# Packed attention followed by a gated MLP on one Trainium2 core: three bursts of small matmul tiles per batch instead of four, and one copy moved ahead of a table load

## The chip, the core and the metric

One core of one Trainium2 chip runs the whole program. The metric is the device time of one execution in microseconds (us). Five engines work side by side, each through its own instruction stream in order: TensorE (PE) multiplies, VectorE (DVE), ScalarE (ACT) and GpSimd (POOL) work elementwise, SyncE (SP) issues DMA transfers; POOL issues some too. They wait for each other by semaphores. PE writes its results to PSUM, which is eight banks of 2 KB in each of 128 partitions; everything else lies in SBUF. Before a weight tile is used PE loads it, which the profile shows as a row of its own (PEld).

## The reference, cut to what matters

```python
batch, n_heads, seq, head_dim, n_pack = 8, 8, 576, 64, 32
n_tokens, d_model, d_ff = 4608, 512, 2048

def sm_attn(qq, kk, vv):
    s = scale * np.matmul(qq, kk.transpose(0, 1, 3, 2))
    s = s - np.max(s, axis=-1, keepdims=True)
    a = np.exp(s)
    a = a / (np.sum(a, axis=-1, keepdims=True) + 1e-09)
    return np.matmul(a, vv)

p_packed = sm_attn(p, k, v)              # 32 packed rows per head
attn = sm_attn(q, p_packed, p_packed)    # every token attends to them
x = attn.transpose(0, 2, 1, 3).reshape(4608, 512)
h = x @ w_in
out = (h * np.cos(h)) @ w_out
```

q, k and v are 8 x 8 x 576 x 64, p is 8 x 8 x 32 x 64, w_in 512 x 2048 and w_out 2048 x 512, all fp32.

## The kernel before

The kernel works batch by batch (B = 8) and computes in bf16 with fp32 sums. It never forms x: since each token's attention output is a weighted sum of 32 packed rows per head, it multiplies the packed rows by w_in first (**PPW**, 256 x 2048 per batch) and then the attention weights by PPW, which gives h directly.

For one batch the steps are, with the helper's name:

- `s1`: scores of p against k, 16 small matmuls (64 rows by 32 columns of the array), and exp with its row sums on ACT. `recips` takes the reciprocals.
- `a1_xbar` (a DMA transpose from SP's queue) or `a1_pe` (PE transposes): the weights transposed.
- `pp` (L173): the packed rows, 48 small matmuls of 96 rows by 32 columns, into one PSUM bank, and two copies of it to `pp_sb`. `pp_T` (L188): two transposes of that and a copy to `ppT`.
- `ppw(b, n)` (L195): chunk n of PPW (512 of its 2048 columns), 8 small matmuls of 64 by 32 into both banks of a PSUM tile, and a copy to SBUF. A batch needs four. `pw2(b, n)` is `ppw(b, n)` and `ppw(b, n + 1)`.
- `s2`: scores of q against the packed rows (16 small matmuls), exp on ACT; `sums2` and `normalise`: row sums by a matmul with ones, their logarithm, exp of the negative, and the product on DVE (`a2n`).
- `h_mm(b, fc)` (L248), for fc = 0 to 15: 128 of the 2048 rows of h. Four full-size matmuls into columns 0 to 287 of both banks of one PSUM tile, cosine on ACT (`Sin` with a bias, L258), product on DVE (L261) into `gT`. It reads PPW chunk fc // 4.
- `out_gen(b)`: the product with w_out, 16 full-size matmuls (L339) for each chunk of 128 tokens. A batch's 576 tokens are four chunks and a half; two halves are put together in `joint` and belong to the odd batch, so an even batch has four chunks and an odd one five. For batch 0 the 64 rest columns of h are done by `h_rest` (L286).

**What sets the order.** Everything is written out by hand in program order (`manual_schedule`); semaphores between engines follow from who reads and writes which tile, and in PSUM by bank. While batch s goes through `h_mm`, the output matmuls of batch s - 1 are dealt out between, as *filler*: `fill(n)` issues the next n of them. `slot(s, hooks, keep, heavy)` (L471) runs the sixteen `h_mm` of a batch. It shares the filler that is left, less `keep`, by weights (1 for each fc, plus what `heavy` adds), and runs the small steps given as hooks at their fc: at a heavy fc half of the quota goes before the hooks and half behind them, elsewhere all of it behind.

**PSUM.** Two banks (`O`, tag ot) are for the output. The other six are `psA`, three tiles of two banks each, which `h_mm`, `ppw`, `s1`, `s2`, `sums2`, `pp` and `pp_T` all draw from by `psa()`; a new tile waits until the last reader of the old one is done. For batch 0 the six banks are single tiles instead (`psH`, by `one()`), used by `h_one` (L274), the variant of `h_mm` with 512 columns.

**ACT's tables.** Exp and logarithm need one table set, Sin another; the kernel loads them by hand (`preload_act_table_set`), twice per batch.

**The parts that the change touches.** The start (L440 to L470): the sixteen `h_one` of batch 0, then `pp_T(1)`, the exp table, three groups of PE transposes of q of batch 1 (`pe_T`, copied by ACT, DVE, DVE), `s2(1)` and what follows. The first slot (L496), the middle between slots 1 and 2 (L506 to L541), the second slot (L542) and the loop over s = 3 to 7 (L545). In the loop small tiles come at four places per batch: `s2(s)` with `ppw(s, 2)`; `s1(s + 1)` with `ppw(s, 3)`; `pp(s + 1)` at fc 5 of the slot; and `pw2(s + 1)`, chunks 0 and 1 of the next batch, at fc 10.

Of the kernel before, what the change touches and what calls it, by code (L numbers as in the profile page):

```python
# [15 lines left out]
def kernel(  # L16
# [18 lines left out]
    HS = S // 2  # L35
# [53 lines left out]
    def psa(dt=FP32):  # L89
        return psum["A"].tile([128, 2, 512 if dt == FP32 else 1024], dt, name="psA", tag="A")  # L90
# [12 lines left out]
    def pe_T(n, b, engs=(V, V, V), groups=(0, 1, 2), own=None):  # L103
        if 0 in groups:
            xT[n, b] = att_pool.tile([128, H * 3, TP], BF16, name=n + "T", tag=n + "T", bufs=2 if n == "k" else 1)
        t = xT[n, b]
        flat = bf[n, b].rearrange("p h x -> p (h x)")
        for i in groups:
            ps = own(BF16) if own else psa(BF16)[:, 0, :]
            for j in range(8):  # L110
                o = 8 * i + j
                nc.tensor.transpose(ps[:, j * TP:(j + 1) * TP], flat[:, o * 128:(o + 1) * 128],
                                    ident[0:TP, 0:TP])
            copy(engs[i], t[:, 8 * i:8 * i + 8].rearrange("p a x -> p (a x)"),
                 ps[:, 0:8 * TP])
# [79 lines left out]
    def ppw(b, n, eng=None, own=False, later=False, cuts=((0, 512),)):  # L195
        if b not in PPW:
            PPW[b] = ppw_pool.tile([128, 2, DF], BF16, name="PPW", tag="PPW")
        two = isinstance(eng, tuple)
        if own:
            ps = [bank(), bank()]  # L200
        else:
            t = psa()
            ps = [t[:, 0, :], t[:, 1, :]]
        for x in range(4):
            for y in range(2):
                r = slice(64 * y, 64 * y + 64)
                nc.tensor.matmul(ps[y][32 * x:32 * x + 32, :], ppT[b % 2][r, 0, x, :],  # L207
                                 w_in_bf[r, x, n * 512:(n + 1) * 512], start=True, stop=True)

        def evacuate(cuts=cuts):  # L210
            if own or two:
                for a, z in cuts:
                    for y in range(2):
                        copy(eng[y] if two else eng, PPW[b][:, y, n * 512 + a:n * 512 + z], ps[y][:, a:z])
            else:
                copy(eng or (V, ACT)[n % 2], PPW[b][:, :, n * 512:(n + 1) * 512], t)
        if later:
            return [lambda c=c: evacuate((c,)) for c in cuts]
        evacuate()
# [25 lines left out]

    gT, joint = {}, {}

    def h_mm(b, fc):  # L248
        if fc == 0:
            g_tile(b)  # L250
        ps = psa()
        for y in range(2):
            for e in range(2):
                nc.tensor.matmul(ps[:, e, 0:HS], PPW[b][:, y, fc * 128:(fc + 1) * 128],  # L254
                                 a2n[b][:, y, e * HS:(e + 1) * HS], start=(y == 0), stop=(y == 1))
        cs = cos_pool.tile([128, S], BF16, name="cosT")
        csv = cs.rearrange("p (e x) -> p e x", e=2)
        ACT.activation(out=csv, in_=ps[:, :, 0:HS], func=AF.Sin, bias=PI_HALF)  # L258

        def rest():  # L260
            V.tensor_tensor(out=gT[b][:, fc, :].rearrange("p (e x) -> p e x", e=2),  # L261
                            in0=ps[:, :, 0:HS], in1=csv, op=ALU.mult)
            if fc % 8 == 7:
                j0 = (b % 2) * 64
                G.tensor_copy(out=joint[b // 2][:, fc - 7:fc + 1, j0:j0 + 64],  # L265
                              in_=gT[b][:, fc - 7:fc + 1, 512:576])
        return rest
# [3 lines left out]
        if b % 2 == 0:  # L271
            joint[b // 2] = j_pool.tile([128, NFC, 128], BF16, name="joint", tag="joint")

    def h_one(b, fc):  # L274

        if fc == 0:
            g_tile(b)
        ps = one()
        for y in range(2):
            nc.tensor.matmul(ps, PPW[b][:, y, fc * 128:(fc + 1) * 128], a2n[b][:, y, 0:512],  # L280
                             start=(y == 0), stop=(y == 1))
        cs = cos_pool.tile([128, 512], BF16, name="cosT")
        ACT.activation(out=cs, in_=ps, func=AF.Sin, bias=PI_HALF)  # L283
        V.tensor_tensor(out=gT[b][:, fc, 0:512], in0=ps, in1=cs, op=ALU.mult)  # L284

    def h_rest(b):  # L286

        t = psa()
        for fc in range(NFC):
            for y in range(2):  # L290
                nc.tensor.matmul(t[:, fc // 8, (fc % 8) * 64:(fc % 8) * 64 + 64],
                                 PPW[b][:, y, fc * 128:(fc + 1) * 128], a2n[b][:, y, 512:576],
                                 start=(y == 0), stop=(y == 1))
        cs = cos_pool.tile([128, 2, 512], BF16, name="cosR", bufs=1)
        ACT.activation(out=cs, in_=t, func=AF.Sin, bias=PI_HALF)
        j0 = (b % 2) * 64
        V.tensor_tensor(out=joint[b // 2][:, :, j0:j0 + 64],
                        in0=t.rearrange("p a (f x) -> p (a f) x", x=64),
                        in1=cs.rearrange("p a (f x) -> p (a f) x", x=64), op=ALU.mult)
# [55 lines left out]
    def fill(n):  # L355
        while n > 0 and filler[1] > 0:
            next(filler[0])
            filler[1] -= 1
            n -= 1
# [13 lines left out]
    def warm(n, wps=None, w=None):  # L373
        wps, w = bank() if wps is None else wps, wz if w is None else w
        for _ in range(n):
            nc.tensor.matmul(wps, w[:, 0:128], w, start=True, stop=True)  # L376
# [61 lines left out]
    a1_pe(1, own=one)  # L438
    recips(1)
    for fc in range(NFC):  # L440
        h_one(0, fc)
        if fc in (0, 4, 8):
            ppw(0, 1 + fc // 4, (ACT, ACT if fc == 8 else V), own=True)
        if fc == 13:
            pp(1, ACT, own=bank)
    warm(2)
    pp_T(1, ACT, own=bank)
    warm(2)
    ACT.preload_act_table_set(EXP_SET)  # L449
    pe_T("q", 1, (ACT, V, V), own=one)  # L450
    warm(4)
    load("v", 2)
    load("q", 2)
# [3 lines left out]
    set_filler(0)  # L457
    s2(1)
    ppw(1, 0, V)
    fill(1)  # L460
    sums2(1, 0)
    fill(1)
    sums2(1, 1)
# [7 lines left out]
    def slot(s, hooks, keep=0, heavy={}):  # L471
        left = filler[1] - keep
        weight = [1 + heavy.get(fc, 0) for fc in range(NFC)]
        for fc in range(NFC):
            h_mm(s, fc)()
            quota = (left * sum(weight[:fc + 1])) // sum(weight) - (left + keep - filler[1])
            first = quota
            while hooks and hooks[0][0] == fc:
                if first == quota and fc in heavy:
                    first = quota // 2  # L480
                    fill(first)
                hooks.pop(0)[1]()
            fill(quota - first if first != quota else quota)

    def pw2(b, n=0, eng=None):
        ppw(b, n, eng)
        ppw(b, n + 1, eng)

    def tk(n, b, i):
        return lambda: pe_T(n, b, (ACT, V, ACT), (i,))  # L490

    def cross(n, b):
        return lambda: xbar(n, b)

    osb_eng[0] = ACT
    slot(1, [(2, lambda: ppw(1, 2, (ACT, V))), (4, lambda: h_rest(0)),  # L496
             (5, lambda: ppw(1, 3, (ACT, V))), (6, lambda: pack_p(2, 4)), (8, tk("k", 2, 0)), (9, tk("k", 2, 1)),
             (9, cross("q", 2)), (10, tk("k", 2, 2)), (12, cross("k", 3))], 4, {4: 2})
    ACT.preload_act_table_set(EXP_SET)
    osb_eng[0] = V  # L500
    G.tensor_copy(out=gate, in_=xT["k", 3][0:1, 0, 0:1])
# [11 lines left out]
    recips(2)  # L513
    fill(5)
    pp(2)
    fill(2)
    pp_T(2)
    s1(3)
    a1_xbar(3)
    recips(3)  # L520
    fill(6)
    s2(2)
# [15 lines left out]
    for n, b in (("v", 4), ("q", 4), ("k", 5)):  # L538
        load(n, b)
    fill(9)  # L540
    osb_eng[0] = ACT  # L541
    slot(2, [(3, lambda: ppw(2, 2, (ACT, V))), (6, lambda: ppw(2, 3, (ACT, V))),  # L542
             (7, lambda: pp(3, ACT)), (8, lambda: pp_T(3, ACT)), (11, lambda: pw2(3))], 5, {11: 3})

    for s in range(3, B):  # L545
        nxt = s + 1 < B
        ACT.preload_act_table_set(EXP_SET)
        osb_eng[0] = V
        fill(1000)
        set_filler(s - 1)  # L550
        s2(s)
        ppw(s, 2, V)
        fill(8)
        if nxt:
            s1(s + 1)
            ppw(s, 3, V)
            a1_xbar(s + 1)
            xbar("q", s + 1)
            recips(s + 1)
            if s + 2 < B:  # L560
                xbar("k", s + 2)
                G.tensor_copy(out=gate, in_=xT["k", s + 2][0:1, 0, 0:1])
        else:
            ppw(s, 3, V)
        fill(4)
        sums2(s, 0)
        fill(5)
        sums2(s, 1)
        normalise(s)
        ACT.preload_act_table_set(SIN_SET)  # L570
        fill(13)
        osb_eng[0] = ACT
        for n, b in (("v", s + 2), ("q", s + 2), ("k", s + 3)):
            if b < B:
                load(n, b)
        slot(s, [(5, lambda: pp(s + 1, ACT)), (6, lambda: pp_T(s + 1, ACT)), (10, lambda: pw2(s + 1))] if nxt else [], 5, {10: 3})
    set_filler(B - 1)
    fill(1000)
    tail_chunk(B - 1, 4)
# [30 lines left out]
```

## Time and profile before

| | us |
|---|---|
| median of 3 runs | 249.57 (249.48 to 250.11) |
| the profiled execution | 249.53 |
| its span, first to last instruction | 247.6 |
| PE busy | 234.0 |
| ACT busy | 170.3 |
| DVE busy | 158.5 |
| matmuls of L339 with gT / joint | 128.2 / 12.6 |
| matmuls of L254 (h) | 73.2 |
| 112 products of L261 on DVE, each | 0.757 |
| 112 cosines of L258 on ACT, each | 0.653 |

The six slots that run `h_mm` in the table below, from the first h matmul of a batch to the start of the next small burst, by the windows view: busy time of each engine in that stretch.

| slot | stretch, us | length | PE | DVE | ACT |
|---|---|---|---|---|---|
| 1 | 40.7 to 62.3 | 21.6 | 21.32 | 15.86 | 15.25 |
| 2 | 76.0 to 95.8 | 19.8 | 19.14 | 16.00 | 15.01 |
| 3 | 104.0 to 121.0 | 17.0 | 16.79 | 13.10 | 14.14 |
| 4 | 129.2 to 149.3 | 20.1 | 19.78 | 13.63 | 14.55 |
| 5 | 157.6 to 174.5 | 16.9 | 16.69 | 13.00 | 14.04 |
| 6 | 182.8 to 202.9 | 20.1 | 19.78 | 13.60 | 14.55 |

How to read it: the granted clock of PE is 1.00 in all of these stretches. Matmuls are pipelined, so a row's duration (0.379 us for a matmul of L339) is longer than the step from one to the next; what a stretch of matmuls costs is read from the start times of the rows in the timeline. In a timeline row the first number is the start, the second how long the group lasted, and the bracket at the end the engine's idle time before it and what ended it.

### The profile page before, as it was taken

The numbers are of one execution on the slowest core, as the hardware profiler recorded it, in microseconds if no ns is written. First come the engines' busy times: TensorE is split into PE (matmuls) and PEld (weight loads), VectorE is DVE, ScalarE is ACT, GpSimd is POOL, SyncE is SP. The second block draws the span as 40 slices with busy tenths as digits, with TensorE's granted clock in tenths as the row PEclk, the third lists the DMA queues.
The fourth block names the chain that finished last, engine by engine and source line by source line (L and its number), as shares of the span: only waits on it lengthen the run. The fifth ranks groups of instructions, "written<-read, shape, count | busy, mean of one in ns | idle before, by whom it ended". The sixth has DMA issues, their size and how long they took to land.

```text
span 247.6 us, 5423 instructions
## 1 busy us (share of the span) xinstructions
PE 234.0 (95%) x2204; PEld 128.3 (52%) x2240; DVE 158.5 (64%) x244; ACT 170.3 (69%) x284; POOL 38.2 (15%) x61
## 2 busy tenths in 40 slices
PE   7988889999989999999999999999999999999993
PEld 3453344566445554565446554565456554665452
DVE  3369977676549777578757666578756685774000
ACT  2369998677568777888787677978886685874110
POOL 8532330200400041005000500030000000000000
PEclk9999999999999999999999999999999999999999
DMA  6999999999899999996999894989292113111123
GB/s 88 204 209 209 202 208 228 202 235 176 135 186 173 218 146 201 189 221 122 215 214 197 148 222 109 184 172 203 63 187 59 42 45 84 43 34 53 52 75 85
DMA packets 63992, 37.37 MB, mean 151 GB/s; under 512 B 36592, under 2 KB 59376, under 8 KB 63968
## 3 DMA queue, kind: packets, MB, share of 16 engines
q0 software_dynamic: 23184, 18.81, 50.0%
q1 hardware_dynamic: 40624, 18.09, 35.6%
q8 instruction: 17, 0.28, 0.5%
q10 hardware_dynamic: 160, 0.13, 0.2%
q14 instruction: 7, 0.06, 0.1%
HBM read 37.22 MB, written 9.44 MB: 188 GB/s over the span
## 4 chain that ended last, share of the span: by engine, by line
PE 82%; DMA 6%; DVE 4%; ACT 3%; issue 2%; POOL 2%; DVEq 0%; ACTq 0%; POOLq 0%
PE ot L339 48%; PE psA L254 22%; DMA w_in_bf<-in_moe_w_in_dram 6%; PE psA L207 3%; PE psA L137 2%; PE ot L325 1%; PE psA L233 1%; PE psA L180 1%; DVE gT L284 1%; PE psH L280 1%; DVE PPW L87 1%; ACT a2u L225 1%; DVE gT L261 1%; POOL kbf L94 1%; ACT L449 1%
## 5 line engine op out<-in xcount | busy, mean ns | idle before, releaser
L339 PE MATMUL ot<-w_out_bf,gT 128*128 128x512 bf16 x482 | 128.2, 379 | 2.8 <-issue 1.9
L261 DVE TENSOR_TENSOR gT<-psA,cosT 128x576 bf16<-128x576 f32 x112 | 83.5, 757 | 32.4 <-ACT cosT L258 31.5
L258 ACT ACTIVATE cosT<-psA 128x576 bf16<-128x576 f32 x112 | 73.0, 653 | 26.4 <-PE psA L254 24.8
L254 PE MATMUL psA<-a2n,PPW 128*128 128x288 bf16 x448 | 73.2, 286 | 0.0
L339 PEld LDWEIGHTS <-gT 128*128 128x128 bf16 x512 | 47.3, 98 | 43.5 <-issue 7.8
L254 PEld LDWEIGHTS <-PPW 128*128 128x128 bf16 x448 | 43.8, 98 | 30.5 <-issue 1.0
L87 DVE CAST PPW<-psA 128x1024 bf16<-128x1024 f32 (+1 forms) x25 | 26.1, 1050 | 7.7 <-PE psA L207 6.0
L87 DVE COPY osb<-ot 128x512 f32<-128x512 f32 (+1 forms) x14 | 9.4, 671 | 21.3 <-PE ot L325 17.4
L85 ACT COPY osb<-ot 128x512 f32<-128x512 f32 (+1 forms) x23 | 13.2, 575 | 13.5 <-PE ot L339 12.4
L265 POOL COPY joint<-gT 128x512 bf16<-128x512 bf16 x14 | 8.6, 617 | 88.4 <-DVE gT L261 88.4
L243 DVE SCALAR_TENSOR_TENSOR a2n<-a2u,r,lns 128x576 bf16<-128x576 bf16 x16 | 12.4, 814 | 8.1 <-ACT lns L241 8.1
L146 ACT ACTIVATE a<-psA 128x576 bf16<-128x576 f32 x16 | 10.3, 646 | 8.3 <-PE psA L137 8.3
L235 ACT ACTIVATE lns<-psA 128x576 f32<-128x576 f32 x16 | 10.3, 651 | 6.5 <-PE psA L233 5.9
L339 PE MATMUL ot<-w_out_bf,joint 128*128 128x512 bf16 x47 | 12.6, 379 | 0.1
L376 PE MATMUL ot<-wz 128*128 128x512 bf16 (+1 forms) x23 | 10.2, 548 | 2.0 <-DVE wz L390 1.7
L225 ACT ACTIVATE a2u<-psA,rs 128x576 bf16<-128x576 f32 x16 | 11.0, 738 | 1.5 <-PE psA L137 1.4
L207 PE MATMUL psA<-w_in_bf,ppT 64*32 64x512 bf16 x224 | 10.4, 380 | 0.2
L284 DVE TENSOR_TENSOR gT<-psH,cosT 128x512 bf16<-128x512 f32 x16 | 9.9, 682 | 0.4 <-ACT cosT L283 0.4
L241 ACT ACTIVATE lns<-lns 128x576 f32<-128x576 f32 x16 | 10.0, 674 | 0.0
L85 ACT CAST PPW<-psA 128x1024 bf16<-128x1024 f32 (+1 forms) x9 | 7.4, 825 | 2.8 <-PE psA L207 2.8
L283 ACT ACTIVATE cosT<-psH 128x512 bf16<-128x512 f32 x16 | 8.7, 619 | 0.9 <-issue 0.4
L280 PE MATMUL psH<-a2n,PPW 128*128 128x512 bf16 x30 | 7.9, 381 | 0.9 <-DVE PPW L87 0.6
(90 smaller groups left out, 163.8 us busy)
## 6 DMA issues: line engine op xcount, KB each, us to landing
kbf<-in_k_dram POOLq DMA_DIRECT2D x8, 576.0 KB, 13.5
vbf<-in_v_dram POOLq DMA_DIRECT2D x8, 576.0 KB, 7.4
qbf<-in_q_dram POOLq DMA_DIRECT2D x8, 576.0 KB, 10.6
out_dram<-osb SPq DMA_DIRECT2D x24, 192.0 KB, 2.8
out_dram<-osb SPq DMA_DIRECT2D x22, 128.0 KB, 2.9
w_in_bf<-in_moe_w_in_dram POOLq DMA_DIRECT2D x4, 512.0 KB, 16.6
w_out_bf<-in_moe_w_out_dram POOLq DMA_DIRECT2D x4, 512.0 KB, 21.2
out_dram<-osb SPq DMA_DIRECT2D x26, 64.0 KB, 2.1
```

The source lines that it names most:

```text
L85: ACT.copy(out=out, in_=in_)
L87: eng.tensor_copy(out=out, in_=in_)
L146: ACT.activation(out=a1[b % 2][:, y, :, 0:TP].rearrange("p (e m) x -> p e m x", e=2), in_=ps[y][:, :, 0:HS].rearrange("p e (m x) -> p e m ...
L207: nc.tensor.matmul(ps[y][32 * x:32 * x + 32, :], ppT[b % 2][r, 0, x, :], w_in_bf[r, x, n * 512:(n + 1) * 512], start=True, stop=True)
L225: ACT.activation(out=a2u[b][:, y].rearrange("p (e x) -> p e x", e=2), in_=ps[y][:, :, 0:HS], func=AF.Exp, scale=rs1[b][:, y:y + 1])
L243: V.scalar_tensor_tensor(out=a2n[b][:, y], in0=a2u[b][:, y], scalar=r1[b][:, y:y + 1], in1=lns[b][:, y], op0=ALU.mult, op1=ALU.mult)
L254: nc.tensor.matmul(ps[:, e, 0:HS], PPW[b][:, y, fc * 128:(fc + 1) * 128], a2n[b][:, y, e * HS:(e + 1) * HS], start=(y == 0), stop=(y == 1))
L258: ACT.activation(out=csv, in_=ps[:, :, 0:HS], func=AF.Sin, bias=PI_HALF)
L261: V.tensor_tensor(out=gT[b][:, fc, :].rearrange("p (e x) -> p e x", e=2), in0=ps[:, :, 0:HS], in1=csv, op=ALU.mult)
L280: nc.tensor.matmul(ps, PPW[b][:, y, fc * 128:(fc + 1) * 128], a2n[b][:, y, 0:512], start=(y == 0), stop=(y == 1))
L284: V.tensor_tensor(out=gT[b][:, fc, 0:512], in0=ps, in1=cs, op=ALU.mult)
L339: nc.tensor.matmul(pss[c], w, w_out_bf[:, fc, :], start=(fc == 0), stop=(fc == NFC - 1))
```

## The change

- In the loop, `ppw(s, 2)` and `ppw(s, 3)` beside `s2(s)` and `s1(s + 1)` become `ppw(s, 0)` and `ppw(s, 1)`. Chunks 2 and 3 of the same batch are computed inside its own slot, at fc 5, right behind `pp(s + 1)`. `pw2(s + 1)` at fc 10 is gone. For the last batch chunks 1 to 3 come one behind the other.
- `pp(s + 1)` in a slot no longer takes a psA tile. It writes into columns 288 to 511 of the second bank of the tile of the newest `h_mm` (`spare`), which `h_mm` leaves unused. `pp_T` moves from fc 6 to fc 7.
- Slot 2 gets the same form, with all of its small tiles at fc 7 and `pp_T` at fc 9. In slot 1 `ppw(1, 2)` and `ppw(1, 3)` are joined at fc 3, `h_rest(0)` moves from fc 4 to fc 6 and `pack_p` from fc 6 to fc 7.
- Between slots 1 and 2, `s1(3)` and `a1_xbar(3)` move from behind `pp_T(2)` to right behind `pp(2)`.
- At the start, group 0 of q of batch 1 is copied by ACT ahead of the exp table's load instead of behind it, and the product of the last `h_one` on DVE comes behind the copies of groups 1 and 2. One more filler matmul goes before `sums2(1, 0)`.

```diff
+    spare = [None]
+
     def h_mm(b, fc):
         if fc == 0:
             g_tile(b)
         ps = psa()
+        spare[0] = ps[:, 1, HS:512]
...
-    def h_one(b, fc):
+    def h_one(b, fc, later=False):
...
-        V.tensor_tensor(out=gT[b][:, fc, 0:512], in0=ps, in1=cs, op=ALU.mult)
+
+        def rest():
+            V.tensor_tensor(out=gT[b][:, fc, 0:512], in0=ps, in1=cs, op=ALU.mult)
+        if later:
+            return rest
+        rest()
...
     for fc in range(NFC):
-        h_one(0, fc)
+        last = h_one(0, fc, fc == NFC - 1)
...
     warm(2)
+    pe_T("q", 1, (ACT, V, V), (0,), own=one)
     ACT.preload_act_table_set(EXP_SET)
-    pe_T("q", 1, (ACT, V, V), own=one)
+    pe_T("q", 1, (ACT, V, V), (1, 2), own=one)
+    last()
     warm(4)
...
     s2(1)
     ppw(1, 0, V)
-    fill(1)
+    fill(2)
     sums2(1, 0)
...
+    def tiled(b, n):
+
+
+        pp(b + 1, ACT, own=lambda: spare[0])
+        pw2(b, n)
+
...
-    slot(1, [(2, lambda: ppw(1, 2, (ACT, V))), (4, lambda: h_rest(0)),
-             (5, lambda: ppw(1, 3, (ACT, V))), (6, lambda: pack_p(2, 4)), (8, tk("k", 2, 0)), (9, tk("k", 2, 1)),
-             (9, cross("q", 2)), (10, tk("k", 2, 2)), (12, cross("k", 3))], 4, {4: 2})
+    slot(1, [(3, lambda: pw2(1, 2, (ACT, V))), (6, lambda: h_rest(0)), (7, lambda: pack_p(2, 4)), (8, tk("k", 2, 0)), (9, tk("k", 2, 1)),
+             (9, cross("q", 2)), (10, tk("k", 2, 2)), (12, cross("k", 3))], 4, {3: 2})
...
     pp(2)
+    s1(3)
+    a1_xbar(3)
     fill(2)
     pp_T(2)
-    s1(3)
-    a1_xbar(3)
...
-    slot(2, [(3, lambda: ppw(2, 2, (ACT, V))), (6, lambda: ppw(2, 3, (ACT, V))),
-             (7, lambda: pp(3, ACT)), (8, lambda: pp_T(3, ACT)), (11, lambda: pw2(3))], 5, {11: 3})
+    slot(2, [(7, lambda: tiled(2, 2)), (9, lambda: pp_T(3, ACT))], 5, {7: 3})
...
         s2(s)
-        ppw(s, 2, V)
+        ppw(s, 0, V)
         fill(8)
         if nxt:
             s1(s + 1)
-            ppw(s, 3, V)
+            ppw(s, 1, V)
...
         else:
-            ppw(s, 3, V)
+            for n in range(1, 4):
+                ppw(s, n, V)
...
-        slot(s, [(5, lambda: pp(s + 1, ACT)), (6, lambda: pp_T(s + 1, ACT)), (10, lambda: pw2(s + 1))] if nxt else [], 5, {10: 3})
+        slot(s, [(5, lambda: tiled(s, 2)), (7, lambda: pp_T(s + 1, ACT))] if nxt else [], 5, {5: 3})
```

## The prediction

> **What bounds the kernel now.** I read the page first: busy shares, then the chain that ended last.
>
> ```profile
> PE 234.0 (95%) x2204; PEld 128.3 (52%) x2240; DVE 158.5 (64%) x244; ACT 170.3 (69%) x284; POOL 38.2 (15%) x61
> PE 82%; DMA 6%; DVE 4%; ACT 3%; issue 2%; POOL 2%; DVEq 0%; ACTq 0%; POOLq 0%
> ```
>
> TensorE is the bound and from 41 us on nothing else is on the chain for long. A gain is therefore an idle gap of PE that closes, a loss is one that opens. To find gaps I compared the start times in the timeline with a clean stream: four 128x288 matmuls of an h chunk take 0.49 us and one output matmul (L339) 0.216 us (five take 1.08). What is over that is a gap. Some L339 records are missing (529 of 560), so a "gap" of 0.22 with a weight load in it is a hidden matmul, not a wait. First the slot of batch 4 (filler of five chunks):
>
> ```profile
> 134.11 0.65 PE L254 MATMUL psA<-a2n,PPW 128*128 128x288 bf16 x4
> 134.69 0.45 PEld L180 LDWEIGHTS <-a1T 96*32 96x32 bf16 x48 [0.24 <-issue]
> 134.80 0.65 ACT L258 ACTIVATE cosT<-psA 128x576 bf16<-128x576 f32 x1 [0.27 <-PE psA L254]
> 135.18 0.33 PEld L339 LDWEIGHTS <-gT 128*128 128x128 bf16 x3
> 135.48 0.76 DVE L261 TENSOR_TENSOR gT<-psA,cosT 128x576 bf16<-128x576 f32 x1 [0.17 <-ACT cosT L258]
> ...
> 89.51 0.63 PE L207 MATMUL psA<-w_in_bf,ppT 64*32 64x512 bf16 x16
> 90.07 0.39 PE L339 MATMUL ot<-w_out_bf,gT 128*128 128x512 bf16 x1
> ```
>
> h(5) is issued by 134.11 + 0.49 = 134.60, pp starts at 134.69: **0.09 to enter** small tiles. pp streams 0.36 and the next full-size work is at 135.19: **0.14 to leave**. pw2 needs 2 x 0.216 = 0.43 and takes 0.56: 0.13 to leave. So a burst costs 0.22 to 0.23 us, and that is all that merging two can return. The second thing to see: Sin starts 0.69 after h(5)'s first matmul and the product ends at 135.48 + 0.76 = 136.24, **2.13 us** after it. pp started at 134.69, long before, because it had a tile of its own.
>
> The slot of batch 3 (filler of four chunks) is tighter:
>
> ```profile
> 107.17 2.98 DVE L261 TENSOR_TENSOR gT<-psA,cosT 128x576 bf16<-128x576 f32 x4 [0.24 <-ACT cosT L258]
> ...
> 108.02 0.65 PE L254 MATMUL psA<-a2n,PPW 128*128 128x288 bf16 x4
> 108.64 0.55 PE L180 MATMUL psA<-vbf,a1T 96*32 96x64 bf16 x48
> ...
> 110.20 0.27 PE L192 MATMUL psA<-ident,pp_sb 128*128 128x128 bf16 x2
> ```
>
> h(5) starts at 108.02 and its product ends at 107.17 + 2.98 = 110.15, again 2.13 later; pp_T, which needs that tile, starts at 110.20. So PE wakes 0.05 after the product.
>
> **The change, part by part.**
>
> *Slots 3 to 6: pp and pw2 become one burst at fc 5.* pp no longer takes a psA tile; it writes into columns 288 to 511 of the second bank of h(5)'s own tile. Sin and the product of h(5) read that bank and stand ahead of pp in the program, so the order between them has to be kept for the bank. The price of this wait lies between nothing (pp at 134.69, a tile of its own) and the full 2.13 + 0.05 = 2.18 us after h(5)'s start (pp_T's row). I take the full one: it is the same bank of the same tile, and h(5) is the newest h, so no earlier product can stand in for it. What covers it is h(5) itself (0.49) and half of the fill quota. The quota follows from the code: with 29 fills over weight 19 it is 6 at fc 5 (half: 3) in slots 3 and 5; with 45 it is 10 (half: 5) in slots 4 and 6. Gap: 2.18 - 0.49 - 0.65 = **1.04** and 2.18 - 0.49 - 1.08 = **0.61**. Behind pp on PE's queue stand pw2, the other half of the fills and h(6); the fills are ready and stand still too, and nothing else feeds PE.
>
> The Trainium skill, "PSUM — Partial Sum Buffer" (PSUM bank collisions raise a hardware error), says software must guard PSUM by bank and quadrant, not by address, since the chip itself doesn't stall. By that rule disjoint columns don't free pp and the sum is 252.1; without the wait it would be 247.3 (below).
>
> Between pp (96*32) and pw2 (64*32) the tile shape changes. No row shows these two shapes side by side. Bounds: 0 (s2 to ppw, same shape, 0.01 at 121.03) to 0.23 (leaving plus entering). I take **0.10**, about one entry.
>
> The Trainium skill, "TensorEngine Tiling (Array Packing)" (Tiling Modes, Key Properties), says a change of tiling mode drains the engine, and lists 128x32 and 64x32 as different modes. It speaks against the merging: with a full drain of 0.23 in six places the sum would be 0.8 higher, 252.9.
>
> After the gap: pp copies, ppw(s,3)'s 1.01 us copy and Sin share ACT, ppw(s,2)'s 1.22 us copy and the products DVE; chunk 2 is copied 2.1 us after pp's start, before h(8). In slots 3 and 5 I walked on with 0.69, 0.65 and 0.76: h(6) 111.84, h(7) 112.76, its pp_T 113.25, one fill, and h(8) would start at 113.58; but pp_T has taken the third tile, and the earliest one back is h(6)'s, product at 113.97: a **0.44** gap, and 0.16 more at h(12). In slots 4 and 6 the larger quotas hide both.
>
> Slots 3 and 5, gaps before: pp 0.09 + 0.05 + 0.14, pp_T 0.15, pw2 0.09 + 0.13, a tile wait 0.16 (116.23 to 116.39) = 0.81. After: 1.04 + 0.10 + 0.13 + 0.44 + 0.16 = 1.87. **+1.06 each.** Slots 4 and 6: before 0.09 + 0.14 + 0.09 + 0.13 = 0.45, after 0.61 + 0.10 + 0.13 = 0.84: **+0.39 each.** Four slots: **+2.90**.
>
> *Slot 2: four bursts become one, at fc 7.* Gaps before add up to 1.50 (four bursts 0.9, tile waits 0.6). After: 2.18 - 0.49 - 4 fills 0.86 = 0.83 for pp; 0.10 + 0.13; then h(8) needs chunk 2, whose matmuls start at 2.64 and whose DVE copy (0.49 later, 1.22 long) ends at 4.35, against 4.07 on PE: 0.33 with the wake-up; 0.23 for h(10)'s tile. 1.62, **+0.12**. Three bursts saved go back into two waits.
>
> *Slot 1: ppw(1,2) and ppw(1,3) join at fc 3, h_rest moves from 4 to 6 and loses its doubled fill, pack_p moves to 7.* Gaps before 0.82. After: one burst 0.22; h_rest holds a tile through 0.93 of matmuls, 1.02 on ACT and 1.23 on DVE with three fills, one h and pack_p behind it, so h(8) waits 0.54, the k transposes 0.26 and 0.16: 1.18, **+0.36**, within 0 and 0.7.
>
> *Start: q1's first group ahead of the exp table.*
>
> ```profile
> 33.23 0.42 ACT L85 COPY ppT<-ot 128x256 bf16<-128x256 bf16 x1
> 33.66 1.28 ACT L449 ACT_TABLE_LOAD   x1
> 34.33 1.01 DVE L87 COPY qT<-psH 128x768 bf16<-128x768 bf16 x2
> 34.95 0.80 ACT L85 COPY qT<-psH 128x768 bf16<-128x768 bf16 x1
> 35.80 0.44 PE L137 MATMUL psA<-qT,ppT 64*32 64x288 bf16 x16 [0.58 <-ACT qT L85]
> 36.24 1.37 ACT L225 ACTIVATE a2u<-psA,rs 128x576 bf16<-128x576 f32 x2 [0.48 <-PE psA L137]
> ```
>
> Before, load, copy, s2 and exp follow each other. After: copy 33.69 to 34.49, load to 35.78, and under the load DVE copies groups 1 and 2 (34.03 to 35.07, ahead of the deferred product) and s2 runs at 35.14. The exp starts at 35.80, 0.44 earlier. The product ends at 35.69 instead; ppw(1,0) needs its bank and starts at 35.74, still before its copy can begin. Sums, the copy that ppw(1,1) waits for, and a2n follow the exp, so h(0) moves by 0.44; fill(2) puts one more 0.216 into PE's idle time there. **-0.65**, between 0 (another wait ends last) and -0.7.
>
> *Middle: s1(3) and a1_xbar(3) ahead of fill(2) and pp_T(2).* pp and s1 become one burst and pp_T's two pp_sb copies are covered. 67.80 to 70.84 is 3.04; the clean sum is pp 0.36, change 0.10, s1 0.24, leaving 0.13, two fills 0.43, pp_T 0.11, six fills 1.29, entry 0.09 = 2.75: **-0.29**. On SP's queue a1_xbar(3) passes the store of chunk 0 of batch 1, which now waits for the exps, about 1.4 us; four osb buffers hide it. POOL's queue is passed by nothing.
>
> *Last batch:* ppw(7,1) to (7,3) in one burst, all copied by DVE. Three 1.23 us copies make sums2(7,0) wait 0.12 and h(0) 0.11: **+0.2**. The total of ppw work is the same.
>
> **Sum:** -0.65 - 0.29 + 0.36 + 0.12 + 2.90 + 0.2 = +2.64. The profiled execution took 249.53 (span 247.6, 1.9 around it): 252.17. Its time is 0.04 below the median of 249.57. I say **252.1**.
>
> **Rivals.**
> 1. *pp does not wait* (the faster side; at pp in slots 2 to 6). For it: the columns are disjoint. Against: the bank is shared with two readers. Then slots 3 and 5 have 0.09 + 0.10 + 0.13 = 0.32 instead of 0.81, slots 4 and 6 0.32 instead of 0.45: -1.24; slot 2 about -0.6; with start, middle, slot 1 and end: -0.65 - 0.29 + 0.36 - 0.6 - 1.24 + 0.2 = -2.2, **247.3**. It decides where the five waits (4.13 together) shrink below 1.5.
> 2. *The wait is there, but the walk's follow-up waits are not* (tiles come back in another order): without 2 x 0.60 and slot 1's 0.36 it is **250.6**.
> 3. *More is lost*: full drain between the shapes (+0.8), or no gain at the start (+0.65): **252.9**.
>
> **From this to the numbers.** Forecast 0.55, rival 2 0.22, rival 3 0.11, rival 1 with its neighbours near 249 0.12. Range 249.5 to 253.2: from the edge of rival 1 to above rival 3. A measurement tells 0.3% (0.75 us) from no change: slower (above 250.3) 0.79, within 0.11 (rival 2 with a full gain at the start), faster 0.10.
>
> **What would show it.** Right: L180 in slots 2 to 6 with 0.6 to 1.0 idle before it, released by DVE gT L261; fewer entries into small tiles, yet a PE idle total 2 to 3 us higher in 76 to 205 us; the exp a2u at 35.8. Wrong: L180 straight behind the fills (rival 1); L180 late but h(8) on time (rival 2); the exp still at 36.2; a gap of 0.2 between the last L180 and the first L207 (rival 3).

## The result, and the profile after

| | before | changed |
|---|---|---|
| median | 249.45 us (249.25 to 250.11, 6 runs) | 252.97 us (252.76 to 253.86, 6 runs) |
| ratio | 1 | 1.0143, interval 1.0124 to 1.0162 |
| profiled execution | 249.53 | 253.86 |
| its span | 247.6 | 252.1 |
| start of pp(1) in it | 30.41 | 31.46 |

The change costs 3.5 us. The two spans lie 4.4 us apart, but 1.05 of that arises ahead of everything that was changed: pp(1) starts at 31.46 instead of 30.41, because in that execution the k transposes waited for their load and started at 17.98 (first row of the timeline fence below; 16.68 in the trace of before, without a wait); two experiments with other edits show the same shift. So executions are compared here by stage, from one start of a row to another, and not by their spans. Two of the 35 executions of the kernel before that ran beside the later four experiments, of 255.86 and 484.56 us, were slow ones and are left out.

The page of the changed kernel, busy times and the chain of waits by engine:

```profile
PE 236.1 (94%) x2240; PEld 128.5 (51%) x2240; DVE 159.7 (63%) x244; ACT 169.0 (67%) x282; POOL 38.1 (15%) x61
PE 78%; DVE 8%; ACT 3%; issue 1%; ACTq 0%; DVEq 0%
```

DVE rose from 4% to 8% of the chain while its busy time grew by 1.2 us only: PE now waits for what DVE does, not for more of it. The view of line 180 (the matmuls of pp), with the idle time of their engine before them, says for which work:

```profile
L180 PE MATMUL psA<-vbf,a1T x336: 189/193/204, 12.3 to 193.6; 96*32 96x64 bf16 x168
...
  issue: 5.8, 11
  DVE gT L264: 3.3, 5
```

Five times pp waited for the product of h on DVE (L264 here, L261 before), in slots 2 to 6. The 3.3 us are idle time behind the modelled ends of the matmuls; from the start times, as the prediction counts, the five gaps add up to 4.14 us. The duration of a matmul is what it was. The timeline of the changed kernel: the load of k, then the start of batch 1, then slot 3 and slot 4, which answer to the two slots shown of before:

```profile
17.98 0.51 PE L112 MATMUL ot<-ident,kbf 96*128 96x96 bf16 x8 [1.01 <-DMA kbf<-in_k_dram]
...
34.57 0.83 ACT L85 COPY qT<-psH 128x768 bf16<-128x768 bf16 x1
34.91 1.02 DVE L87 COPY qT<-psH 128x768 bf16<-128x768 bf16 x2
...
35.42 1.28 ACT L458 ACT_TABLE_LOAD   x1
...
35.85 0.68 DVE L289 TENSOR_TENSOR gT<-psH,cosT 128x512 bf16<-128x512 f32 x1
...
36.68 0.44 PE L137 MATMUL psA<-qT,ppT 64*32 64x288 bf16 x16 [0.60 <-DVE gT L289]
...
37.11 1.37 ACT L225 ACTIVATE a2u<-psA,rs 128x576 bf16<-128x576 f32 x2 [0.41 <-PE psA L137]
...
107.79 2.98 DVE L264 TENSOR_TENSOR gT<-psA,cosT 128x576 bf16<-128x576 f32 x4 [0.25 <-ACT cosT L261]
...
109.13 0.81 PE L347 MATMUL ot<-w_out_bf,gT 128*128 128x512 bf16 x3
...
110.82 0.55 PE L180 MATMUL psA<-vbf,a1T 96*32 96x64 bf16 x48 [0.88 <-DVE gT L264]
...
111.30 0.62 PE L207 MATMUL psA<-w_in_bf,ppT 64*32 64x512 bf16 x16
...
112.52 0.65 PE L257 MATMUL psA<-a2n,PPW 128*128 128x288 bf16 x4
...
113.54 1.29 ACT L261 ACTIVATE cosT<-psA 128x576 bf16<-128x576 f32 x2 [0.53 <-PE psA L257]
...
114.04 0.38 PE L347 MATMUL ot<-w_out_bf,gT 128*128 128x512 bf16 x1
...
114.23 1.42 DVE L264 TENSOR_TENSOR gT<-psA,cosT 128x576 bf16<-128x576 f32 x2 [1.22 <-ACT cosT L261]
...
115.04 0.65 PE L257 MATMUL psA<-a2n,PPW 128*128 128x288 bf16 x4 [0.62 <-DVE gT L264]
...
136.51 1.24 PE L347 MATMUL ot<-w_out_bf,gT 128*128 128x512 bf16 x5
...
137.40 0.76 DVE L264 TENSOR_TENSOR gT<-psA,cosT 128x576 bf16<-128x576 f32 x1 [0.17 <-ACT cosT L261]
...
138.21 0.55 PE L180 MATMUL psA<-vbf,a1T 96*32 96x64 bf16 x48 [0.45 <-DVE gT L264]
```

Slot 3: three fills from 109.13 take 0.65 and end at 109.78; the products end at 107.79 + 2.98 = 110.77; pp starts at 110.82. The gap is 1.04. Slot 4: five fills from 136.51 take 1.08, the product ends at 138.16, pp starts at 138.21: 0.62. From pp to pw2 it is 111.30 - 110.82 = 0.48, where the 48 matmuls of pp start within 0.35: the change of tile shape costs 0.13. Then one fill from 114.04 takes 0.22 and h(8) starts at 115.04, 0.78 late, released by the product of h(6).

By stage, in us, each from the start of one row to the start of another (s2 is the first L137 of a batch's s2):

| stage | before | changed | change | predicted |
|---|---|---|---|---|
| pp(1) to h(0) of batch 1 | 10.31 | 10.19 | -0.12 | -0.43 |
| h(0) to s1(2), slot 1 | 22.70 | 22.69 | -0.01 | +0.14 |
| s1(2) to s2(2), middle | 7.42 | 7.18 | -0.24 | -0.29 |
| s2(2) to h(0) of batch 2 | 5.14 | 5.13 | -0.01 | 0 |
| slot 2, to s2(3) | 19.82 | 19.77 | -0.05 | -0.31 |
| s2(3) to s2(4) | 25.23 | 26.53 | +1.30 | +1.06 |
| s2(4) to s2(5) | 28.35 | 28.82 | +0.47 | +0.39 |
| s2(5) to s2(6) | 25.22 | 26.25 | +1.03 | +1.06 |
| s2(6) to s2(7) | 28.34 | 28.82 | +0.48 | +0.39 |
| s2(7) to the end | 44.68 | 45.21 | +0.53 | +0.63 |
| sum | | | +3.38 | +2.64 |

The last column is the prediction's terms by the stage in which the time shows them: the fill of 0.216 that moves from slot 1 to the start, and the 0.43 of PPW matmuls that move from slot 2 to the last batch, are put where they move. The sum of 3.38 fits the medians (252.97 - 249.45 = 3.52). The first row depends on when pp(1) came: in the four experiments that have the changed start and an early pp(1), at 30.36 to 30.55 as before, that stage took 10.34 to 10.39, no less than before, and the sum would be 3.53 to 3.58.

### The profile page after: what moved, and what is told of

Same layout as the page of the kernel before. It is cut to its first block, busy times and chain, and to the rows that moved or that the text cites. A ratio compares the mean times of both kernels' runs of the same rounds, so it can differ in the third digit from the quotient of the medians.

```text
span 252.1 us, 5464 instructions
## 1 busy us (share of the span) xinstructions
PE 236.1 (94%) x2240; PEld 128.5 (51%) x2240; DVE 159.7 (63%) x244; ACT 169.0 (67%) x282; POOL 38.1 (15%) x61
## 4 chain that ended last, share of the span: by engine, by line
PE 78%; DVE 8%; ACT 3%; issue 1%; ACTq 0%; DVEq 0%
PE ot L347 45%; PE psA L257 21%; DVE gT L264 3%; PE psA L207 3%; ACT cosT L261 2%; DVE PPW L87 2%; PE psA L137 2%; DVE gT L289 1%; PE ot L333 1%; PE psH L283 1%; PE psA L180 1%; PE psA L233 1%; ACT a2u L225 1%; PE psA L112 1%; DVE joint L305 0%
## 5 line engine op out<-in xcount | busy, mean ns | idle before, releaser
L347 PE MATMUL ot<-w_out_bf,gT 128*128 128x512 bf16 x512 | 132.9, 379 | 0.0
L264 DVE TENSOR_TENSOR gT<-psA,cosT 128x576 bf16<-128x576 f32 x112 | 83.2, 757 | 32.2 <-ACT cosT L261 31.2
L261 ACT ACTIVATE cosT<-psA 128x576 bf16<-128x576 f32 x112 | 72.7, 653 | 26.0 <-PE psA L257 24.4
L87 DVE CAST PPW<-psA 128x1024 bf16<-128x1024 f32 (+1 forms) x25 | 26.9, 1094 | 13.4 <-PE psA L207 11.7
L289 DVE TENSOR_TENSOR gT<-psH,cosT 128x512 bf16<-128x512 f32 x16 | 10.0, 685 | 0.4 <-ACT cosT L286 0.4
L207 PE MATMUL psA<-w_in_bf,ppT 64*32 64x512 bf16 x224 | 9.8, 379 | 0.2 <-DVE PPW L87 0.2
L180 PEld LDWEIGHTS <-a1T 96*32 96x32 bf16 x384 | 4.0, 96 | 6.7 <-issue 5.8
```

The source lines that it names most:

```text
L87: eng.tensor_copy(out=out, in_=in_)
L347: nc.tensor.matmul(pss[c], w, w_out_bf[:, fc, :], start=(fc == 0), stop=(fc == NFC - 1))
```

## Experiments

The eight runs are told by what they ask. All ratios are against the kernel before, run on the same chip: 249.76 us (22 runs) beside the first four, 249.65 us (33 runs) beside the other four.

**Does pp wait for the bank, or only stand late?** The same order of work, but pp in a psA tile of its own in slots 2 to 6:

```diff
-        pp(b + 1, ACT, own=lambda: spare[0])
+        pp(b + 1, ACT)
```

> The changed kernel, but pp in the slots takes a psA tile of its own again instead of the free columns of h(5)'s tile (h(7)'s in slot 2); pw2 stays right behind it. Theory (the loss is pp's wait for the product of the newest h, whose bank it shares): pp starts 0.09 behind the fills as in the kernel before; only the third tile of the burst, for the second ppw, still has to wait for that product, about 0.24 in slots 3 and 5 and not at all in 4 and 6. Gaps around the burst fall from 1.30 to 0.59 (slots 3, 5), from 0.88 to 0.35 (4, 6) and by about 0.65 in slot 2: 3.1 us less in all, give or take 0.6 for later tile waits, so 249.9 us. Rival (the loss comes from chunks 2 and 3 made late and from three tiles taken in a row): a third tile makes that worse, 253.0 or more.

Measured: 249.5 us (249.09 to 251.18), ratio 0.9988, interval 0.9965 to 1.001. The loss is gone. Slot 3 in its timeline:

```profile
107.52 0.81 PE L347 MATMUL ot<-w_out_bf,gT 128*128 128x512 bf16 x3
...
108.26 0.56 PE L180 MATMUL psA<-vbf,a1T 96*32 96x64 bf16 x48
...
109.21 0.11 PEld L207 LDWEIGHTS <-ppT 64*32 64x32 bf16 x7 [0.36 <-issue]
...
109.55 0.33 PEld L347 LDWEIGHTS <-gT 128*128 128x128 bf16 x3 [0.23 <-issue]
...
112.40 0.65 PE L257 MATMUL psA<-a2n,PPW 128*128 128x288 bf16 x4 [0.28 <-DVE gT L264]
```

Three fills end at 108.17 and pp starts 0.09 later: no wait. But now pp, ppw and ppw take all three tiles in a row. The second ppw starts late (the weight loads at 109.21 after 0.36 of idle), and pw2 lasts 0.81 (108.74 to 109.55) instead of 0.55 (111.30 to 111.85 in the changed kernel's trace). h(8) still starts 0.44 late. The wait has moved and shrunk, from 1.04 to 0.26.

**Is it the shared bank or the newest product?** pp in the spare columns of the tile of the h before, whose product ends one step earlier:

```diff
-        spare[0] = ps[:, 1, HS:512]
+        spare[:] = [spare[-1], ps[:, 1, HS:512]]
```

> The changed kernel, but pp writes into the free columns of the tile of the h before the newest one (h(4); h(6) in slot 2). It still shares a bank with a Sin and a product. Theory (the newest product is what is late, sharing a bank costs nothing by itself): that product is done 1.26 (slots 4, 6) to 1.47 us (3, 5) after h(5)'s start, so pp waits 0.24 in slots 3 and 5 and not at all elsewhere; as many gaps as with a tile of its own, 249.9 us. Rival (sharing a bank with other engines slows pp or the readers): the rows of L180, L261 or L264 get longer and most of the loss stays, 252 or more.

Measured: 250.31 us (249.58 to 252.38), ratio 1.0019, interval 0.9993 to 1.0045. Sharing a bank as such costs little: in slots 3 and 5 the gap at pp is 0.34 instead of 1.04, in slots 4 and 6 it is 0.09 instead of 0.61 (nothing but the entry). Slot 2 gained nothing in the profiled execution, and its timeline says why:

```profile
82.63 1.03 PE L347 MATMUL ot<-w_out_bf,gT 128*128 128x512 bf16 x4
...
84.47 0.45 PEld L180 LDWEIGHTS <-a1T 96*32 96x32 bf16 x48 [1.31 <-DMA a1T<-a]
84.47 0.56 PE L180 MATMUL psA<-vbf,a1T 96*32 96x64 bf16 x48 [0.82 <-DMA a1T<-a]
```

Here pp waited for the DMA transpose of its own weights, a second gate close behind the first.

**Can filler cover the wait?** At a heavy fc of slots 2 to 6 all but one of the quota goes ahead of the burst:

```diff
-                    first = quota // 2
+                    first = quota // 2 if s < 2 else quota - 1
```

> The changed kernel, but in slots 2 to 6 all of the heavy fc's fills but one go ahead of pp, and one behind (5 and 1 in slots 3 and 5, 9 and 1 in 4 and 6, 7 and 1 in 2). The work and its dependencies are the same. Theory (wait for the newest product): pp's idle time falls from 1.04 to 0.61 in slots 3 and 5, from 0.61 to nothing in 4 and 6, from 0.83 to 0.18 in 2; in 2, 3 and 5 most of it comes back as a longer wait of h(8), since ACT and DVE still start from the same moment. Net about -0.2 for each of slots 3 and 5, -0.5 for each of 4 and 6, nothing in 2: 251.6 us. Rival (the burst itself, by its shape changes, costs the time): the order of the fills changes nothing, 253.0.

Measured: 251.88 us (251.4 to 252.87), ratio 1.008, interval 1.0054 to 1.0107. Less than half of the loss comes back. At pp the filler covers what it should (gap 0.61 in slots 3 and 5, 0.18 in slot 2, 0.09 in slots 4 and 6), which is 2.56 us less over the five slots; by stage they get back 1.68. Most of what is missing is missing in slot 2, behind the burst. Its timeline:

```profile
84.43 0.55 PE L180 MATMUL psA<-vbf,a1T 96*32 96x64 bf16 x48
...
84.91 0.63 PE L207 MATMUL psA<-w_in_bf,ppT 64*32 64x512 bf16 x16
...
85.39 1.23 DVE L87 CAST PPW<-psA 128x1024 bf16<-128x1024 f32 x1 [1.01 <-PE psA L207]
85.46 0.10 PEld L347 LDWEIGHTS <-gT 128*128 128x128 bf16 x1 [0.42 <-issue]
...
86.67 0.66 PE L257 MATMUL psA<-a2n,PPW 128*128 128x288 bf16 x4 [1.14 <-DVE PPW L87]
```

h(8) needs chunk 2, whose copy ends at 86.62. pp came earlier in its slot, the copy with it, and yet h(8) waits longer, since the fills that stood before it are used up. The 1.14 in the row holds the one fill that is left (its weight load is at 85.46, its matmul record is missing): 84.91 + 0.56 + 0.22 = 85.69, so the wait is 0.98 instead of 0.34. Slot 2 gains 0.65 at pp and loses 0.64 at h(8): it lasts 19.76, as in the changed kernel (19.77).

**What did deferring the product do?** The changed kernel with the last product of h(0) in its place, ahead of the q copies:

```diff
-        last = h_one(0, fc, fc == NFC - 1)
+        h_one(0, fc)
...
-    last()
```

> The changed kernel, but the product of the last h_one of batch 0 stays in its place ahead of the copies of q1's groups 1 and 2; group 0 is still copied ahead of the exp table's load. Theory (s2(1) waits for the deferred product, so that the start gains only a third of what the moved copy could give): s2 starts when the two copies end, the exp starts about 0.2 us sooner behind the table's load, and the kernel takes 252.8 us. Rival (the copies on DVE end last in either order): the copies end 0.6 later, the exp starts at the same time or later, 253.0 to 253.4.

Measured: 253.1 us (252.71 to 253.36, 4 runs), ratio 1.0117, interval 1.0081 to 1.0152. The times can't tell this from the changed kernel, and the number lies in the rival's range. The trace speaks for the theory: s2(1) starts 4.89 after pp(1) instead of 5.22, h(0) 9.86 instead of 10.19 (5.41 to 5.42 and 10.37 to 10.39 in the three profiles of this chip with the deferral and a pp(1) as early as here). Slot 1 then lasts 22.86 instead of 22.69, so 0.17 of it is lost again.

**Where does the loss sit?** The changed kernel with slot 2 and the loop of before (the hooks of slot 2 and of `slot(s, ...)`, `ppw(s, 2)` and `ppw(s, 3)` beside s2 and s1):

```diff
-    slot(2, [(7, lambda: tiled(2, 2)), (9, lambda: pp_T(3, ACT))], 5, {7: 3})
+    slot(2, [(3, lambda: ppw(2, 2, (ACT, V))), (6, lambda: ppw(2, 3, (ACT, V))),
+             (7, lambda: pp(3, ACT)), (8, lambda: pp_T(3, ACT)), (11, lambda: pw2(3))], 5, {11: 3})
...
-        ppw(s, 0, V)
+        ppw(s, 2, V)
...
-        slot(s, [(5, lambda: tiled(s, 2)), (7, lambda: pp_T(s + 1, ACT))] if nxt else [], 5, {5: 3})
+        slot(s, [(5, lambda: pp(s + 1, ACT)), (6, lambda: pp_T(s + 1, ACT)), (10, lambda: pw2(s + 1))] if nxt else [], 5, {10: 3})
```

> The changed kernel with slot 2 and the loop over slots 3 to 7 as before; start, middle and slot 1 stay changed. Theory: the loss of 3.5 us is in the slots put back, and what stays is -0.33 - 0.23 + 0.20 = -0.4: 249.1. Rival (slot 1's bunching costs the 0.36 predicted or more): 249.3 to 249.6. If the changed slots are not the cause, it stays near 253.

Measured: 249.58 us (249.35 to 250.06), ratio 0.9992, interval 0.9978 to 1.0006. Slots 2 to 6 and the last batch are the whole loss. The number is the rival's, but not for its reason: slot 1 took 22.69, no longer than before (22.70). What is left by stage, -0.13 at the start (with a late pp(1), at 31.20), -0.01 in slot 1 and -0.24 in the middle, is too small for the times to show.

**What are the other parts worth?** The kernel before with the start and the middle of the change alone:

```diff
+    pe_T("q", 1, (ACT, V, V), (0,), own=one)
     ACT.preload_act_table_set(EXP_SET)
-    pe_T("q", 1, (ACT, V, V), own=one)
+    pe_T("q", 1, (ACT, V, V), (1, 2), own=one)
+    last()
...
-    fill(1)
+    fill(2)
...
+    s1(3)
+    a1_xbar(3)
     fill(2)
     pp_T(2)
-    s1(3)
-    a1_xbar(3)
```

> The kernel before, with two parts of the change alone: q1's first group ahead of the exp table with the last product deferred and fill(2), and s1(3) with a1_xbar(3) ahead of fill(2) and pp_T(2). All slots are those of before. Theory (the loss sits in the slots, the other parts gain what the profiles of before and after show, 0.33 at the start and 0.23 in the middle): 249.5 - 0.56 = 248.9. Rival (these parts are worth what the prediction said, 0.65 and 0.29): 248.6. Second rival (the profile's start was a matter of its run and the parts are worth nothing): 249.5.

Measured: 249.6 us (249.26 to 250.25), ratio 1.0001, interval 0.9986 to 1.0016: the theory was wrong. The middle gained its 0.24, the start nothing (10.34), and slot 1, with one fill less to do, became longer, not shorter: 22.81 against 22.70.

The same without the deferral, so without `last()`:

> As the run with start and middle alone, but the last product of h(0) stays in its place ahead of the q copies, so that s2(1) finds its psA tile back while the table loads. Theory (the deferral takes back 0.32 of the start's gain): 249.5 - 0.65 - 0.23 = 248.6, 0.3 below the same with the deferral. Rival (a2n or the q transposes end last instead, as one profile showed): 0.1 to 0.2 below it, 248.8. In the trace s2(1) should start before the load has ended.

Measured: 249.35 us (248.87 to 249.82), ratio 0.9979, interval 0.9959 to 0.9999. That is above the theory and its rival, but it is the one version whose interval lies below 1, if only just. By stage: start 9.95 (-0.36), slot 1 22.81 (+0.11), middle 7.19 (-0.23), the rest as before, in sum -0.48 us; the ratio says 0.5. Its timeline at the start:

```profile
34.53 1.01 DVE L87 COPY qT<-psH 128x768 bf16<-128x768 bf16 x2
...
34.73 1.28 ACT L450 ACT_TABLE_LOAD   x1
...
35.60 0.44 PE L137 MATMUL psA<-qT,ppT 64*32 64x288 bf16 x16 [0.17 <-DVE qT L87]
...
36.03 1.37 ACT L225 ACTIVATE a2u<-psA,rs 128x576 bf16<-128x576 f32 x2
```

s2(1) now waits for the q copies (34.53 + 1.01 = 35.54) and starts under the table load, which ends at 36.01; the exp starts at 36.03 with no idle time before it. The load sets the time, as the prediction wanted.

**Is merging worth anything once nothing waits?** The changed kernel with pp in its own tile, the product in its place and slot 1 as before (the first two edits are shown above, the third undoes the change of `slot(1, ...)`):

> The changed kernel with pp in a psA tile of its own in slots 2 to 6, the last product of h(0) in its place, and slot 1 as before: the bursts merged where merging costs no wait on the newest product. Theory: 249.5 (the run with the own tile) - 0.3 (deferral) - 0.2 (slot 1) = 249.0. Rival (merging alone is worth the 0.22 us of each burst saved, in seven places): 247.5 to 248. If merging is worth nothing once pp takes a third tile, it is no better than start and middle alone without the deferral.

Measured: 249.39 us (248.64 to 250.6), ratio 0.9987, interval 0.9967 to 1.0008. That is above the theory, far from the rival, and no better than the run before it, which has all the bursts of the kernel before.

The stages of slots 2 to 6 side by side; where two programs share a stage, their profiles agree within 0.03:

| stage | before | changed | fills ahead | older tile | own tile |
|---|---|---|---|---|---|
| slot 2 | 19.82 | 19.77 | 19.76 | 19.92 | 18.97 |
| s2(3) to s2(4) | 25.23 | 26.53 | 26.09 | 25.82 | 25.48 |
| s2(4) to s2(5) | 28.35 | 28.82 | 28.39 | 28.31 | 28.25 |
| s2(5) to s2(6) | 25.22 | 26.25 | 25.89 | 25.54 | 25.48 |
| s2(6) to s2(7) | 28.34 | 28.82 | 28.38 | 28.31 | 28.25 |
| s2(7) to the end | 44.68 | 45.21 | 45.21 | 45.20 | 45.20 |

Own tile against changed, slots 2 to 6: 0.80 + 1.05 + 0.57 + 0.77 + 0.57 = 3.76 us. That is the price of putting pp into a bank that was still being read, and more than the whole loss. Own tile against before: -0.85 + 0.25 - 0.10 + 0.26 - 0.09 + 0.52 = -0.01. Three bursts instead of four come out at nothing here: what they save in slots 2, 4 and 6 goes back in slots 3 and 5, where three tiles in a row have to wait for one.

## Why the prediction was right, and where it was off

The forecast was slower, 252.1, in a range of 249.5 to 253.2; the median is 252.97. The sum was 0.74 too low by stage. Some luck is in that: start, middle, slot 2 and the stages of slots 3, 4 and 6 came out 1.03 worse than forecast, and slot 1, slot 5 and the last batch 0.29 better.

**The wait at pp: right in place, releaser and size.** Predicted gaps were 1.04 (slots 3 and 5), 0.61 (slots 4 and 6) and 0.83 (slot 2). Measured: 1.04 twice, 0.62 and 0.61, and 0.83 (four fills from 83.53 take 0.86, pp at 85.22). The reading behind it was that the newest product ends 2.13 after its h starts, and PE wakes 0.05 later.

The rule of the Trainium skill, "PSUM — Partial Sum Buffer" (PSUM bank collisions raise a hardware error), that order has to be kept by bank and not by address, agrees with these gaps of 0.6 to 1.04: disjoint columns didn't free pp. What is seen here is the semaphore that kept this order; no run leaves it out, so none shows that the chip needs it.

**The follow-up wait: right in kind, too small.** h(8) was to wait 0.44 in slots 3 and 5 for the third tile. It waited 0.78 and 0.50, for the product of h(6) as predicted. In slot 3 the cosine of h(6) starts 113.54 - 112.52 = 1.02 after the first of its matmuls instead of the 0.69 that the prediction took, with ACT idle; slot 5 has 168.61 - 167.86 = 0.75. Nothing that it is seen to wait for ends in these 0.33 us. The older-tile run and the run with the product in place show 1.03 at the same instruction; what it is stays open. h(12), predicted 0.16 late, was 0.02 late. Slots 4 and 6 were to hide the wait whole and left 0.07 and 0.03.

**The change of tile shape: 0.13, where I took 0.10.** It lies between the bounds of 0 and 0.23, and far from the full drain of the third rival.

The Trainium skill, "TensorEngine Tiling (Array Packing)" (Tiling Modes, Key Properties), says that a change of mode drains the engine; the rows agree that there is a price, and it is 0.13, less than the 0.22 of leaving and entering.

With it the return of merging can be read: a merged pair saves 0.22 and pays 0.13, so 0.09 is left, and slots 4 and 6 of the own-tile run gained 0.10 and 0.09.

**Slot 2: mis-sized by 0.26.** I had 0.33 at h(8) and 0.23 at h(10) and found 0.34 and 0.29, but another 0.15 ahead of the burst (78.78 + 0.43 to 79.36, a gap that the kernel before has too and that the sum left out) and 0.03 more at the shape change.

**The start: the step that failed.** The prediction let the deferred product end at 35.69 and named only ppw(1,0) as waiting for its bank, "still before its copy can begin". The row of L137 shows the error: s2(1) itself takes the tile, `[0.60 <-DVE gT L289]`, and starts behind the product instead of under the table load. The exp came 37.11 - 31.46 = 5.65 after pp(1) instead of 36.24 - 30.41 = 5.83, a gain of 0.18 where 0.44 was predicted. Even that goes with the late pp(1) of this execution: in the four experiments with this start and an early pp(1) the exp came 5.80 to 5.85 after it, no gain at all. Undoing the deferral (start and middle alone, product in place) gives 36.03 - 30.61 = 5.42, a gain of 0.41: the table load was the right target, and the deferral stood in its way.

**The extra fill: worth nothing.** I credited 0.216 for a fill done in idle time. With start and middle alone, old slot 1 became 0.11 longer with one fill fewer, instead of 0.22 shorter. In its timeline the h at 54.21 is followed by the k transposes at 55.03, 0.82 for 0.49 of work (before: 54.03 to 54.63, 0.60): a fill that is not there doesn't cover a wait for a tile.

**Slot 1: mis-sized the other way.** I had +0.36. With one fill fewer than before, the changed slot 1 took 22.69 and the old order 22.81, so the joined ppw is worth -0.12: a wait at the k transposes, which the prediction charged to the new order, is in the old one too once the fill is gone (0.82 - 0.49 = 0.33).

**Middle and last batch** came out at -0.24 and +0.53, for -0.29 and +0.63 predicted. The whole time is near that of the third rival (252.9), but not by its full drain; its other reason, no gain at the start, is true in four of the six profiles with this start and in part in the other two. The first rival was wrong, the second held for h(12) and slot 1 alone.

## What to carry to other kernels

Columns of a PSUM bank that nobody used were not free here while other engines read the rest of the bank: before a writer goes there, ask when the last reader ends, and compare that with the cost of what it saves (here 3.76 us paid for a merging worth 0.09 us a burst). Before an operation is deferred, list everybody who waits for the buffer that it holds, the next allocation from the same banks too. And count filler by what it covers, not by its own time: moved ahead of pp in slot 2 it opened a gap of the same size behind the burst, and taken out of slot 1 it left a wait there uncovered.

## What the runs showed of the hardware

- Between 96-row and 64-row tiles of the same 32 columns PE lost 0.13 us in every one of the merged bursts; entering small tiles from full-size ones cost 0.09.
- The same DMA transpose of a1T for slot 2 took 11.6 us from issue to landing before and in the changed kernel, 13.1 with the product in place, 14.3 in the older-tile run, where it became the gate of pp, and 10.6 to 11.9 in the other six profiles. A transfer that looks hidden in one trace took up to 2.7 us longer in another.
- The waits for the load of k at 16 to 18 us were there or not from execution to execution and moved pp(1) between 30.4 and 31.5 us; two single executions of programs that are the same up to there can so differ by 1 us.
- The 0.33 us by which one cosine in slot 3 started late, in three programs at the same place, has no releaser in the trace but its own matmuls, which were done.
